# Grouped score products, a pinned TensorE order and slot weights spread by DMA in a fused Nyström attention and soft mixture-of-experts kernel

## The chip, the cores and the metric

One NeuronCore of a Trainium2 chip runs the whole kernel. The metric is device time in microseconds (us) of that core. The engines have names that the profile shortens: PE is TensorE (matrix products), PEld its weight loads, DVE is VectorE, ACT is ScalarE, POOL is GpSimd, SP is SyncE, which issues the DMAs. PSUM is the memory that TensorE writes; it has eight banks, and here each tile in it takes one bank.

## The reference, cut to what matters

```python
# q, k, v: (8 batches, 8 heads, 576 tokens, 64)
q_lm, k_lm = means of q and k over 32 segments of 18 tokens
A, Bm, C = sm(q, k_lm), sm(q_lm, k_lm), sm(q_lm, k)
Z = Bm.T / (norms of Bm)
for _ in range(6): Z = 2 * Z - Z @ Bm @ Z
x = A @ Z @ C @ v                       # then (8*576, 512)
g = x @ w_gate
x = (g * sigmoid(g) * (x @ w_val)) @ w_out
logits = x @ phi                        # 32 slots
d = softmax(logits, axis=0); slot_input = d.T @ x
slot_out[e] = relu(slot_input[e] @ w1[e]) @ w2[e]
out = softmax(logits, axis=1) @ slot_out
```

## The kernel before, in words

The eight batches run one after the other. In each, the feed-forward part dominates: for 12 blocks `j` of 128 hidden channels and 2 halves of 288 tokens, `unit` (L906) forms one gate group `pg` and one value group `pv` of six products each (`mm3`, L897: high and low halves of `E`, the softmax of A, times those of `G`). ACT turns `pg` into `u` (L917, L920), DVE multiplies `u` by `pv` into `hT` (L930, L932) and transposes `hT` into the big buffer `HB` (L761). `g_product` (L702) forms the `G` of two blocks at a time from `WB` and the weights: two PSUM tiles of tag "x", which ACT casts into `GH` (L727) and DVE subtracts into `GL` (L741).

Around these groups, work of other kinds is placed by slots. A batch has 48 slots, four per block `j`: after pg of half 0, after pv of half 0, after pg of half 1, after pv of half 1. In the second of the four (slot number 4j + 1) the `G` product of the next pair, where one is due, and the logits `l` of the previous block (L756) are always placed. Four generators are advanced at the slots which the lists in `SCHED` give them:

- `attention(b)` (L532, lists at1, at2, at3) prepares batch b during batch b - 1, so a negative slot lies in the batch before that. It has 34 steps: eight landmark sums on DVE (`landmark`, L319: four of k into `ks`, then four of q into `qs`), with the loads of the next q or k issued on SP after the fourth of each; four evictions of the A scores `m_a` by DVE (L547); four of the C scores `m_c` by ACT (L560); maxima and exponentials (L571 to L579); transposes `m_t` (L594 to L603); the product with v, `m_v` (L613); six steps of the Newton iteration, `m_n` (L634 to L658); and `m_w`, which gives `WB` (L519), after POOL has added the identity to `bd` (L659). q and k share four buffers: k is loaded for its landmarks, then q for landmarks and A scores, then k again for the C scores.
- `a_softmax(b)` (L664, lists am1 to am3) is the softmax of A, on DVE, POOL and ACT.
- `softmoe(b)` (L792, list sm) does the slot softmax of batch b during batch b + 1. Its weights `DN` lie transposed, and every group of 32 partitions needs those of all four groups. L839 to L844 spread them by eight recorded products `m_dr` into PSUM and by copies of DVE and ACT into `DR`. Then 144 small products `m_d` (L872) sum the tokens into four PSUM tiles (three of tag "x", one of tag "pv"), which DVE adds to `Sacc` (L882); these additions set a fence, and landmarks that come after them in the program wait for it.

The PSUM banks are three of tag "x", two of "pg", two of "pv" and one "l". In `attention` the scores of each half are one group: two "x" tiles, 16 products, two evictions (L541 to L561). So A and C scores stand in four places.

The framework's planner sets the order of instructions on each engine at compile time. It takes the earliest of the program that is ready by its own estimates, so work is moved ahead of the program's order where it expects an engine to be free. On the chip each engine then goes through its instructions in that fixed order. `issue_after` keeps an instruction behind another on its engine. `in_order` (L295) keeps exponentials and SiLUs apart, as a change between them loads an activation table; the halves in `TANH` (L939), which lie between the exponentials, use tanh instead.

The batch before the first (`first_attention`, L351) and the tail from L1091 on, the experts' products and the output, stand apart.

Of the kernel before, what the change touches and what calls it, by code (L numbers as in the profile page):

```python
# [19 lines left out]
M = 32  # L20
# [3 lines left out]
HALF = S // 2  # L24
NE, FF = 8, 1024
SEG = S // M
# [27 lines left out]
def nystrom_softmoe_kernel(  # L54
# [13 lines left out]
):  # L68
    nc = tc.nc
    pe, act, dve, pool, sp = nc.tensor, nc.scalar, nc.vector, nc.gpsimd, nc.sync  # L70

    def open_pool(name, bufs=1, **kw):
        return ctx.enter_context(tc.tile_pool(name=name, bufs=bufs, **kw))
# [30 lines left out]
    DN = cp.tile([128, 5, M], F32, name="DN")  # L104
# [188 lines left out]
    fence = {}  # L293
# [45 lines left out]
        E_t[b] = r  # L339

    def attention_tiles(b):
        ks = ap.tile([128, 4, M], F32, tag="ks", name="ks")
        qs = ap.tile([128, 4, M], F32, tag="qs", name="qs")
        if b != 1:
            e_tiles(b)
        AN = [ap.tile([128, SEG, M], F32, tag=f"AN{q}", name=f"AN{q}") for q in range(2)]
        A_t[b] = (AN, ap.tile([128, 2, SEG], F32, tag="mxA", name="mxA"))
        CE = [ap.tile([128, S + M], F32, tag=f"CE{q}", name=f"CE{q}") for q in range(2)]
        return ks, qs, AN, CE

    def first_attention(side):  # L351
        b = 0
        ks, qs, AN, CE = attention_tiles(b)
        NBUF = big("w5", "newton").rearrange("p (i q m) -> p i q m", q=2, m=128)
        am = [[psp.tile([128, 512], F32, tag=("pg", "pv")[half], name="m_a", bufs=2) for r in range(2)]
              for half in range(2)]
# [173 lines left out]
                          qk_t[nm, b, hp][64 * r:64 * r + 64, HALF * half:HALF * half + HALF], start=True, stop=True)  # L530

    def attention(b):  # L532
        assert b == 1 or ("att", b - 1) in seq
        ks, qs, AN, CE = attention_tiles(b)
        for nm, dst in (("k", ks), ("q", qs)):
            for hp in range(4):
                (landmark_pool if b == 1 and S_["lp"][2 * hp + (nm == "q")] else landmark)(nm, b, hp, dst)
                if hp == 3 and b > 1:
                    load_four("q" if nm == "k" else "k", b)
                yield  # L540
        for half in range(2):  # L541
            ms = [psp.tile([128, 512], F32, tag="x", name="m_a", bufs=3) for r in range(2)]
            scores(ms, ks, "q", b, half, range(4))
            assert b == 1 or ("asm", b - 1) in seq
            seq.add(("A", b, half))
            for r in range(2):
                dve.transpose(AN[r][:, 9 * half:9 * half + 9, :], ms[r][:, 0:HALF].rearrange("p (t r) -> p t r", r=32))  # L547
                yield
        for half in range(2):
            ms = [psp.tile([128, 512], F32, tag="x", name="m_c", bufs=3) for r in range(2)]  # L550
            scores(ms, qs, "k", b, half, range(4))
            n = HALF
            if half:
                n += M
                for hp in range(4):
                    for r in range(2):
                        pe.matmul(ms[r][32 * hp:32 * hp + 32, HALF:n], qs[64 * r:64 * r + 64, hp, :],
                                  ks[64 * r:64 * r + 64, hp, :], start=True, stop=True)
            for r in range(2):
                act.copy(CE[r][:, HALF * half:HALF * half + n], ms[r][:, 0:n])  # L560
                yield  # L561
        if b == 1:
            e_tiles(b)
        elif b < nb - 1:
# [5 lines left out]
        for q in range(2):  # L570
            dve.tensor_reduce(stat[:, q, 0:1], CE[q][:, 0:S], axis=AX.X, op=ALU.max)  # L571
            dve.tensor_reduce(stat[:, q, 1:2], CE[q][:, S:S + M], axis=AX.X, op=ALU.max)
            dve.tensor_scalar(stat[:, q, 2:3], stat[:, q, 0:1], -SC / SEG, None, ALU.mult)
            dve.tensor_scalar(stat[:, q, 3:4], stat[:, q, 1:2], -SC / (SEG * SEG), None, ALU.mult)
            yield
            in_order("exp", CE[q][:, 0:S], CE[q][:, 0:S], AF.Exp, bias=stat[:, q, 2:3], scale=SC / SEG,
                           accum_out=stat[:, q, 4:5])
            in_order("exp", CE[q][:, S:S + M], CE[q][:, S:S + M], AF.Exp, bias=stat[:, q, 3:4],
                           scale=SC / (SEG * SEG), accum_out=stat[:, q, 5:6])  # L579
            yield  # L580
# [83 lines left out]
    def a_softmax(b, qs=(0, 1)):  # L664
        EH, EL = E_t[b]
        AN, mxA = A_t[b]

        assert b == 0 or ("A", b, 1) in seq
        bc = {q: mxA[:, q, :].unsqueeze(2).to_broadcast([128, SEG, M]) for q in qs}
        at = {}  # L670

        def inv(q):
            mx = mxA[:, q, :]
            dve.tensor_reduce(mx, AN[q], axis=AX.X, op=ALU.add)
            dve.tensor_scalar(mx, mx, 1e-9, None, ALU.add)
            dve.reciprocal(mx, mx)

        def back(q):
            at[q] = ap.tile([128, S], F32, tag="AT", name="AT", bufs=2)
            dve.transpose(at[q].rearrange("p (t r) -> p t r", r=32), AN[q])  # L680

        for f in (lambda q: dve.tensor_reduce(mxA[:, q, :], AN[q], axis=AX.X, op=ALU.max),  # L682
                  lambda q: pool.tensor_tensor(out=AN[q], in0=AN[q], in1=bc[q], op=ALU.subtract),  # L683
                  lambda q: in_order("exp", AN[q], AN[q], AF.Exp, scale=SC / SEG),
                  inv,
                  lambda q: pool.tensor_tensor(out=AN[q], in0=AN[q], in1=bc[q], op=ALU.mult),
                  back,
                  lambda q: act.copy(EH[:, q, :], at[q]),
                  lambda q: pool.tensor_tensor(out=EL[:, q, :], in0=at[q], in1=EH[:, q, :], op=ALU.subtract)):
# [102 lines left out]
    def softmoe(b):  # L792
# [43 lines left out]
        room = spare[(b + 1) % 2]  # L836
        if b < nb - 1:
            DR = room[:, 0:640].rearrange("p (g k s) -> p g k s", g=4, k=5)
            for g in range(4):  # L839
                m = psp.tile([128, 512], F32, tag="x", name="m_dr", bufs=3)  # L840
                pe.matmul(m[:, 0:160], msum[32 * g:32 * g + 32, :],
                          DN[32 * g:32 * g + 32].rearrange("p k s -> p (k s)"), start=True, stop=True)
                o = DR[:, g].rearrange("p k s -> p (k s)")
                act.copy(o, m[:, 0:160]) if g % 2 else dve.tensor_copy(o, m[:, 0:160])  # L844
            d_of = lambda a, g, k: DR[32 * a:32 * a + 32, g, k, :]
        else:

# [39 lines left out]
            if a == 0:  # L887
                yield
        yield
        dve.tensor_reduce(mx, c, axis=AX.X, op=ALU.add)  # L890
        dve.tensor_scalar(mx, mx, 1e-9, None, ALU.add)
        dve.reciprocal(mx, mx)
        dve.tensor_tensor(out=c, in0=c, in1=bc, op=ALU.mult)
        yield


# [39 lines left out]

    WARM = [3, 4, 3, 2, 2]

    TANH = {(4, 1), (5, 0), (5, 1)}  # L939
    GROUPS = [2, 2, 4, 8, 8, 8, 4]  # L940


# [82 lines left out]
    def tail_loads(b, n):  # L1025
# [3 lines left out]
            for t in range(NW):  # L1029
                ffn_prefetch(t)  # L1030
        if b == last:
            if n == 25:
                for t in range(NW, NW + 3):
                    ffn_prefetch(t)
            if n % 8 == 6:
# [9 lines left out]
    for a in range(1, nb):  # L1045
# [5 lines left out]
        for r in S_["sm"]:  # L1051
            todo[48 * a + r].append(sm)
    prev = None
    for b in range(nb):
        for j in range(NJ):
            p = prev
            def slot(i):
# [24 lines left out]
                if not first:  # L1082
                    for gen in todo[48 * b + n]:
                        next(gen, None)
                if n == 46 and b + 1 < nb:
                    g_unit(b + 1, 0)
                if n == 47:
                    g_low()

            prev = (b, j, *unit(b, j, slot))  # L1090
    in_order("exp", warm, one, AF.Exp)  # L1091
    logits(*prev)
    transposes(*prev)
# [205 lines left out]
```

## Time and profile before

| | |
|---|---|
| time of the kernel, median of 3 runs | 687.33 us (687.18 to 689.19) |
| time of the profiled execution | 688.07 us |
| its span, first to last instruction | 686.3 us |
| PE busy | 641.6 us, 93% |
| DVE busy | 484.5 us, 71% |
| ACT busy | 307.2 us, 45% |
| POOL busy | 72.2 us, 11% |
| mean granted TensorE clock | 0.985 of 2.4 GHz |

Busy time of PE counts each product from its start to its modelled end, and products overlap in the pipeline. So the time that a group costs is read from the start of its first product to the start of the next group, and a small gap inside "busy" does not show as idle. The time of the profiled execution is 1.77 us over its span and 0.74 us over the median.

### The profile page before, as it was taken

What the parts mean: (1) busy time and instruction counts of PE and PEld (TensorE: products, weight loads), DVE (VectorE), ACT (ScalarE), POOL (GpSimd) and SP (SyncE); (2) the same over time, 40 slices, a digit from 0 to 9 for tenths busy, and PEclk for the clock granted to TensorE, in tenths of its full rate; (3) what the DMA queues carried; (4) which work ended last, traced back from release to release, by engine and by line L of the source; (5) the groups of instructions that cost most, each with busy time, mean ns of one, the idle gap of its engine ahead of it and who ended that gap; (6) DMA issues with size and microseconds to landing.
All of it is one profiled execution on the core that took longest, in us unless ns stands there. A gap on an engine that the chain in (4) does not pass through costs nothing.

```text
span 686.3 us, 18326 instructions
## 1 busy us (share of the span) xinstructions
PE 641.6 (93%) x7639; PEld 470.2 (69%) x7639; DVE 484.5 (71%) x1166; ACT 307.2 (45%) x776; POOL 72.2 (11%) x81
## 2 busy tenths in 40 slices
PE   5699999999999999999999999999999999989991
PEld 2576767776877687777777777777768886843560
DVE  4999989878657985798569856976696655550441
ACT  2566875356335533463246324632364342321441
POOL 0401012012001200120012001200130000010000
PEclk9799999999999999999999999999999999999996
DMA  7788773232203230224022402240212296789999
GB/s 283 258 323 316 279 269 119 83 126 84 70 1 96 72 114 2 72 82 126 1 71 71 140 1 70 72 139 1 71 63 63 77 367 227 249 268 351 348 369 326
DMA packets 59843, 105.01 MB, mean 153 GB/s; under 512 B 3824, under 2 KB 29552, under 8 KB 58224
## 3 DMA queue, kind: packets, MB, share of 16 engines
q1 hardware_dynamic: 59760, 103.84, 45.0%
q8 instruction: 60, 0.98, 0.6%
q14 instruction: 23, 0.19, 0.1%
HBM read 91.24 MB, written 12.58 MB: 151 GB/s over the span
## 4 chain that ended last, share of the span: by engine, by line
PE 68%; DVE 17%; ACT 6%; DMA 4%; issue 2%; POOL 1%; SPq 0%; POOLq 0%; ACTq 0%; DVEq 0%
PE pg L903 20%; PE pv L903 17%; PE g L710 6%; PE l L756 4%; PE m_n L637 3%; PE m_d L872 3%; PE m_f L1232 2%; PE m_f L1184 2%; PE m_a L529 2%; DMA q<-in_qT_dram 2%; DMA v<-in_v_dram 2%; DVE bd L311 2%; DVE GL L741 1%; DVE Sacc L882 1%; DVE qs L322 1%
## 5 line engine op out<-in xcount | busy, mean ns | idle before, releaser
L301 ACT ACTIVATE u<-pg 128x288 f32<-128x288 f32 x174 | 71.4, 411 | 143.8 <-PE pg L903 138.7
L932 DVE TENSOR_TENSOR hT<-u,pv 128x288 f32<-128x288 f32 x174 | 78.2, 450 | 56.9 <-PE pv L903 51.3
L903 PE MATMUL pg<-EH,GH 128*128 128x288 f32 x384 | 96.9, 330 | 2.5 <-ACT GH L727 1.6
L741 DVE TENSOR_TENSOR GL<-g,GH 128x512 fp32r<-128x512 f32 (+1 forms) x122 | 66.0, 571 | 38.7 <-ACT GH L727 38.5
L903 PE MATMUL pv<-EH,GH 128*128 128x288 f32 x384 | 91.2, 312 | 0.5 <-DVE hT L932 0.5
L903 PE MATMUL pg<-EH,GL 128*128 128x288 f32 x384 | 86.0, 299 | 0.0
L903 PE MATMUL pg<-EL,GH 128*128 128x288 f32 x384 | 84.0, 298 | 0.0
L903 PE MATMUL pv<-EH,GL 128*128 128x288 f32 x384 | 83.1, 295 | 0.0
L903 PE MATMUL pv<-EL,GH 128*128 128x288 f32 x384 | 82.7, 296 | 0.0
L727 ACT CAST GH<-g 128x512 fp32r<-128x512 f32 (+1 forms) x122 | 54.2, 496 | 56.4 <-PE g L710 56.3
L903 PEld LDWEIGHTS pg<-EH,GH 128*128 128x128 f32 x384 | 59.9, 189 | 25.3 <-issue 20.3
L761 DVE STREAM_TRANSPOSE HB<-hT 128x576 f32<-128x576 f32 x96 | 73.9, 770 | 1.3
L903 PEld LDWEIGHTS pv<-EH,GH 128*128 128x128 f32 x384 | 61.4, 188 | 18.0 <-issue 16.2
L903 PEld LDWEIGHTS pg<-EH,GL 128*128 128x128 f32 x384 | 62.3, 188 | 2.2 <-issue 2.1
L903 PEld LDWEIGHTS pg<-EL,GH 128*128 128x128 f32 x384 | 61.6, 188 | 1.8 <-issue 1.8
L903 PEld LDWEIGHTS pv<-EL,GH 128*128 128x128 f32 x384 | 61.6, 188 | 0.9 <-issue 0.9
L903 PEld LDWEIGHTS pv<-EH,GL 128*128 128x128 f32 x384 | 61.9, 188 | 0.5 <-issue 0.5
L710 PE MATMUL g<-w,WB 64*32 64x512 f32 (+1 forms) x976 | 56.5, 510 | 0.4 <-ACT WB L523 0.4
L756 PE MATMUL l<-hT,P_sb 128*32 128x128 f32 (+1 forms) x768 | 47.4, 298 | 0.7 <-DVE hT L932 0.6
L756 PEld LDWEIGHTS l<-hT,P_sb 128*32 128x32 f32 x768 | 15.9, 108 | 40.3 <-issue 17.8
L872 PE MATMUL m_d<-HB,HB 32*32 32x384 f32 x1116 | 39.5, 491 | 0.3 <-DVE GL L741 0.3
L683 POOL TENSOR_TENSOR AN<-AN,mxA 128x576 f32<-128x576 f32 x16 | 18.4, 1170 | 179.6 <-DVE mxA L682 163.3
(248 smaller groups left out, 945.2 us busy)
## 6 DMA issues: line engine op xcount, KB each, us to landing
k<-in_kT_dram SPq DMA_DIRECT2D x52, 288.0 KB, 3.8
ffn<-in_w_dram SPq DMA_DIRECT2D x13, 1024.0 KB, 8.7
ffn<-in_w_dram SPq DMA_DIRECT2D x24, 512.0 KB, 8.8
HB<-in_w_cat_dram SPq DMA_DIRECT2D x8, 1024.0 KB, 7.8
v<-in_v_dram SPq DMA_DIRECT2D x8, 1024.0 KB, 6.0
q<-in_qT_dram SPq DMA_DIRECT2D x28, 288.0 KB, 3.2
HB<-in_w_out_dram SPq DMA_DIRECT2D x12, 512.0 KB, 5.8
wr<-in_w_cat_dram SPq DMA_DIRECT2D x4, 1024.0 KB, 9.4
```

The costliest lines, as they stand in the source:

```text
L301: i = act.activation(*a, **kw)
L311: dve.tensor_tensor(out=dst[:, q, :].rearrange("p (h m) -> p h m", h=4), in0=src.unsqueeze(1).to_broadcast([128, 4, 32]), in1=bm3, op=ALU. ...
L637: pe.matmul(m[:, 96 * q:96 * q + 96], bd[:, q, :], RV[:, q, :], start=True, stop=True)
L683: lambda q: pool.tensor_tensor(out=AN[q], in0=AN[q], in1=bc[q], op=ALU.subtract),
L710: pe.matmul(gs[r][32 * hp:32 * hp + 32, 0:256 * n].rearrange("p (u f) -> p u f", u=n), WB[b % 2][64 * r:64 * r + 64, hp, :], w[64 * r:64 * ...
L727: act.copy(H_, g)
L741: dve.tensor_tensor(out=GL, in0=g, in1=GH, op=ALU.subtract)
L756: pe.matmul(L[32 * c:32 * c + 32, 0:32 * k], P_sb[:, j, :], main[:, 0:k, c, :], start=j == 0, stop=j == NJ - 1)
L761: dve.transpose(HB[b % 2][:, S * j:S * j + S].rearrange("p (t r) -> p t r", r=32), hT[:, 0:S].rearrange("p (t r) -> p t r", r=32))
L872: pe.matmul(ms[a][32 * g:32 * g + 32, 0:384].rearrange("p (j f) -> p j f", j=NJ), d_of(a, g, k), hb[32 * a:32 * a + 32, :, 4 * k + g, :], ...
L903: pe.matmul(ps[:, 0:HALF], G_t[b, j, q, sel_][h], e[:, q, ts_], start=n == 0, stop=n == 5)
L932: dve.tensor_tensor(out=o, in0=u, in1=pv[:, 0:HALF], op=ALU.mult)
```

## The change

The score products of both halves of A are formed in one group of 32, and those of C likewise, for batches from 2 on; the fourth PSUM tile is taken from tag "pv" and evicted first. The order of all PE instructions from batch 1 to the end of batch 7 is tied to the program's order (`keep_order`). In `softmoe` of batches 0 to 5, twelve DMAs on SP copy `DN` into `DR`, and the group that a partition already holds is read from `DN`; `softmoe(6)` keeps the products. The slots of nearly all steps change; landmarks of batches from 3 on may begin before the attention of the batch before has ended; the first `G` product of the next batch moves from slot 46 to 45; the tanh halves move with the exponentials. Two fences are added on DVE.

```diff
-    'at2': [-3, -2, -1, 0, 3, 4, 5, 6, 8, 8, 10, 10, 16, 16, 18, 18, 19, 20, 20, 21, 22, 23, 25, 26, 27, 28, 29, 31, 33, 35, 37, 39, 41, 43],
-    'am2': [11, 11, 12, 12, 18, 19, 21, 22, 23, 25, 27, 29, 31, 32, 34, 36, 37],
-    'at3': [-3, -2, -1, 0, 3, 4, 5, 6, 8, 8, 10, 10, 16, 16, 18, 18, 19, 20, 20, 21, 22, 23, 25, 26, 27, 28, 29, 31, 33, 35, 37, 39, 41, 43],
-    'am3': [11, 11, 12, 12, 18, 19, 21, 22, 23, 25, 27, 29, 31, 32, 34, 36, 37],
-    'sm': [1, 3, 10, 17, 19, 20, 23, 24, 24, 27],
+    'at2': [-3, -2, -1, 0, 1, 2, 3, 4, 5, 6, 6, 7, 9, 10, 10, 11, 11, 12, 13, 13, 14, 14, 17, 17, 17, 18, 21, 23, 24, 28, 30, 32, 34, 37],
+    'am2': [7, 7, 8, 8, 12, 13, 15, 16, 17, 19, 21, 23, 25, 27, 29, 31, 33],
+    'at3': [-11, -10, -9, -8, -5, -4, -3, -2, 1, 2, 2, 3, 9, 10, 10, 11, 11, 12, 13, 13, 14, 14, 17, 17, 17, 18, 21, 23, 24, 28, 30, 32, 34, 37],
+    'am3': [6, 7, 7, 8, 12, 13, 15, 16, 17, 19, 21, 23, 25, 27, 29, 31, 33],
+    'sm': [2, 3, 5, 9, 10, 10, 25, 26, 26, 28],
...
+    def keep_order(engine, start, end):
+        last = None
+        for i in nc.cur_bb.bb.instructions[start:end]:
+            if i.engine == engine:
+                if last is not None:
+                    tc.add_manual_dep(i, last.name, mybir.DependencyInfo(
+                        mybir.DependencyClass.NoSync, mybir.DependencyReason.DATA), reason="keep_order")
+                last = i
...
     def attention(b):
-        assert b == 1 or ("att", b - 1) in seq
+        assert b == 1 or ("q", b - 1) in seq
...
+        def score_tiles(name):
+            ms = [psp.tile([128, 512], F32, tag="pv" if i == 3 else "x", name=name, bufs=2 if i == 3 else 3)
+                  for i in (3, 0, 1, 2)]
+            return {(1, 1): ms[0], (0, 0): ms[1], (0, 1): ms[2], (1, 0): ms[3]}
+        together = b > 1
...
+            if together:
+                t = score_tiles(name)
+                for half in (1, 0):
+                    product(half, [t[half, 0], t[half, 1]])
+                for half, r in ((1, 1), (0, 0), (0, 1), (1, 0)):
+                    eviction(half, r, t[half, r])
+                    yield
...
-            dve.tensor_scalar(stat[:, q, 3:4], stat[:, q, 1:2], -SC / (SEG * SEG), None, ALU.mult)
+            i = dve.tensor_scalar(stat[:, q, 3:4], stat[:, q, 1:2], -SC / (SEG * SEG), None, ALU.mult)
+            fence["stat"] = getattr(i, "ins", i)
...
-            dve.tensor_reduce(mx, AN[q], axis=AX.X, op=ALU.add)
+            with tc.issue_after(fence["stat"]) if b > 1 else nullcontext():
+                dve.tensor_reduce(mx, AN[q], axis=AX.X, op=ALU.add)
...
-            for g in range(4):
+            for i in range(1, 4 if b < nb - 2 else 1):
+                for a in range(4):
+                    sp.dma_start(DR[32 * a:32 * a + 32, a ^ i], DN[32 * (a ^ i):32 * (a ^ i) + 32])
+            for g in range(4 if b == nb - 2 else 0):
                 m = psp.tile([128, 512], F32, tag="x", name="m_dr", bufs=3)
...
-            d_of = lambda a, g, k: DR[32 * a:32 * a + 32, g, k, :]
+            d_of = lambda a, g, k: (DN if a == g else DR[:, g])[32 * a:32 * a + 32, k, :]
...
-        dve.tensor_reduce(mx, c, axis=AX.X, op=ALU.add)
...
+        with tc.issue_after(fence["sum"]):
+            dve.tensor_reduce(mx, c, axis=AX.X, op=ALU.add)
...
-    TANH = {(4, 1), (5, 0), (5, 1)}
+    TANH = {(2, 1), (3, 0), (3, 1)}
...
-            if n == 25:
+            if n == 26:
                 for t in range(NW, NW + 3):
                     ffn_prefetch(t)
...
-                if n == 46 and b + 1 < nb:
+                if n == (46 if b == 0 else 45) and b + 1 < nb:
                     g_unit(b + 1, 0)
-                if n == 47:
+                if n == (47 if b == 0 else 46):
                     g_low()
...
+    keep_order(mybir.EngineType.PE, middle, n_ins())
```

## Rows read from the trace of the kernel before

**Rows 1.** The chain that ended last: start us, us, what; a batch apart

```profile
217.27 1.28 ACT L301
...
287.02 1.28 ACT L301
...
356.94 1.28 ACT L301
...
506.65 4.95 PE m_d L872 x141
...
571.22 4.25 PE m_d L872 x141
```

**Rows 2.** Busy time by engine in the stretch of one batch

```profile
core 0: us, PE busy (x) PEld busy (x) DVE busy (x) ACT busy (x) POOL busy (x), PEclk, DMA share, GB/s
...
287.02:356.94 69.92, 68.65 (x842) 51.97 (x832) 53.30 (x129) 30.69 (x79) 8.25 (x8) 1.00 0.22 69
```

**Rows 3.** Waits of PE, 224 to 502 us: us in total, times, longest

```profile
PE m_n L637 <- ACT RV L644: 2.8, 4, 0.8
PE m_w L522 <- POOL bd L659: 1.5, 4, 0.4
```

**Rows 4.** Timeline of PE, 354.7 to 358.5 us: start, us, engine, line, operation

```profile
354.73 0.43 PE L903 MATMUL pv<-EH,GH 128*128 128x288 f32 x2
...
355.52 0.43 PE L903 MATMUL pg<-EH,GH 128*128 128x288 f32 x2
...
356.41 0.71 PE L529 MATMUL m_c<-k,qs 64*32 64x288 f32 x16
357.05 0.53 PE L903 MATMUL pv<-EH,GH 128*128 128x288 f32 x2
...
358.05 0.47 PE L756 MATMUL l<-hT,P_sb 128*32 128x160 f32 x8
358.44 0.53 PE L903 MATMUL pg<-EH,GH 128*128 128x288 f32 x2
```

**Rows 5.** Timeline of PE around the spread of the slot weights

```profile
292.24 0.55 PE L841 MATMUL m_dr<-DN,cst 32*128 32x160 f32 x6
...
293.20 0.53 PE L841 MATMUL m_dr<-DN,cst 32*128 32x160 f32 x2
...
294.52 1.09 PE L710 MATMUL g<-w,WB 64*32 64x512 f32 x16
```

**Rows 6.** Timeline of PE at the end of a batch

```profile
334.11 1.09 PE L710 MATMUL g<-w,WB 64*32 64x512 f32 x16
335.13 0.53 PE L903 MATMUL pv<-EH,GH 128*128 128x288 f32 x2
...
339.67 0.42 PE L903 MATMUL pv<-EH,GH 128*128 128x288 f32 x2
```

**Rows 7.** Timeline of PE, Newton steps and the product after them

```profile
316.31 0.47 PE L756 MATMUL l<-hT,P_sb 128*32 128x160 f32 x8
317.58 0.66 PE L637 MATMUL m_n<-RV,bd 128*128 128x96 f32 x4 [0.80 <-ACT RV L644]
...
319.70 0.58 PE L637 MATMUL m_n<-RV,bd 128*128 128x96 f32 x4
...
330.84 0.44 PE L522 MATMUL m_w<-bd,VD 128*64 128x128 f32 x4 [0.36 <-POOL bd L659]
```

**Rows 8.** Timeline of DVE beside these steps

```profile
311.76 1.50 DVE L322 TENSOR_REDUCE qs<-q 128x32 f32<-128x576 f32 x2 [0.48 <-DMA q<-in_qT_dram]
...
318.27 0.49 DVE L311 TENSOR_TENSOR bd<-m_n,cst 128x128 f32<-128x128 f32 x2 [0.28 <-PE m_n L637]
...
319.10 0.29 DVE L653 TENSOR_TENSOR RV<-RV,m_n 128x128 f32<-128x128 f32 x1 [0.33 <-ACT RV L652]
```

**Rows 9.** Timeline of SP: one load of k as four DMAs

```profile
290.50 1.75 SPq L149 DMA_DIRECT2D k<-in_kT_dram  x4
```

**Rows 10.** DMA issues: times, KB each, median us to landing

```profile
k<-in_kT_dram SPq DMA_DIRECT2D x52, 288.0 KB, 3.8
```

**Rows 11.** Groups by line, whole kernel: the evictions of the A scores

```profile
L547 DVE STREAM_TRANSPOSE AN<-m_a 128x288 f32<-128x288 f32 x28 | 11.9, 463 | 11.7 <-PE m_a L529 11.7
```

More of the change, by code (lines that the diff above doesn't have):

```diff
@@ L341, in attention_tiles @@
     def attention_tiles(b):
[L342 to L345, printed above, removed]
         AN = [ap.tile([128, SEG, M], F32, tag=f"AN{q}", name=f"AN{q}") for q in range(2)]
@@ L348, in attention_tiles, with landmark_tiles @@
         CE = [ap.tile([128, S + M], F32, tag=f"CE{q}", name=f"CE{q}") for q in range(2)]
-        return ks, qs, AN, CE
+        return AN, CE
+    def landmark_tiles():
+        return ap.tile([128, 4, M], F32, tag="ks", name="ks"), ap.tile([128, 4, M], F32, tag="qs", name="qs")
     def first_attention(side):
         b = 0
-        ks, qs, AN, CE = attention_tiles(b)
+        ks, qs = landmark_tiles()
+        e_tiles(b)
+        AN, CE = attention_tiles(b)
         NBUF = big("w5", "newton").rearrange("p (i q m) -> p i q m", q=2, m=128)
@@ L532, in attention @@
     def attention(b):
-        assert b == 1 or ("att", b - 1) in seq
-        ks, qs, AN, CE = attention_tiles(b)
+        assert b == 1 or ("q", b - 1) in seq
+        ks, qs = landmark_tiles()
         for nm, dst in (("k", ks), ("q", qs)):
@@ L540, in attention @@
                 yield
[L541 to L550, printed above, removed]
+        def score_tiles(name):
+            ms = [psp.tile([128, 512], F32, tag="pv" if i == 3 else "x", name=name, bufs=2 if i == 3 else 3)
+                  for i in (3, 0, 1, 2)]
+            return {(1, 1): ms[0], (0, 0): ms[1], (0, 1): ms[2], (1, 0): ms[3]}
@@ L551, in attention, with a_eviction, c_product @@
+        together = b > 1
+        assert b == 1 or ("att", b - 1) in seq and ("asm", b - 1) in seq
+        AN, CE = attention_tiles(b)
+        if b != 1:
+            e_tiles(b)
+        def a_eviction(half, r, m):
+            dve.transpose(AN[r][:, 9 * half:9 * half + 9, :], m[:, 0:HALF].rearrange("p (t r) -> p t r", r=32))
+            if (half, r) == (1, 0 if together else 1):
+                seq.add(("A", b, 1))
+        def c_product(half, ms):
             scores(ms, qs, "k", b, half, range(4))
-            n = HALF
@@ L553, in attention, with c_eviction @@
             if half:
-                n += M
                 for hp in range(4):
                     for r in range(2):
-                        pe.matmul(ms[r][32 * hp:32 * hp + 32, HALF:n], qs[64 * r:64 * r + 64, hp, :],
+                        pe.matmul(ms[r][32 * hp:32 * hp + 32, HALF:HALF + M], qs[64 * r:64 * r + 64, hp, :],
                                   ks[64 * r:64 * r + 64, hp, :], start=True, stop=True)
-            for r in range(2):
-                act.copy(CE[r][:, HALF * half:HALF * half + n], ms[r][:, 0:n])
-                yield
+        def c_eviction(half, r, m):
+            n = HALF + M * half
+            act.copy(CE[r][:, HALF * half:HALF * half + n], m[:, 0:n])
@@ new lines, in attention @@
+        for name, product, eviction in (
+                ("m_a", lambda half, ms: scores(ms, ks, "q", b, half, range(4)), a_eviction),
+                ("m_c", c_product, c_eviction)):
+            if together:
[5 more added lines that the diff above has]
+                    yield
+            else:
+                for half in range(2):
+                    ms = [psp.tile([128, 512], F32, tag="x", name=name, bufs=3) for r in range(2)]
+                    product(half, ms)
+                    for r in range(2):
+                        eviction(half, r, ms[r])
+                        yield
@@ L889, in softmoe @@
         yield
-        dve.tensor_reduce(mx, c, axis=AX.X, op=ALU.add)
-        dve.tensor_scalar(mx, mx, 1e-9, None, ALU.add)
-        dve.reciprocal(mx, mx)
-        dve.tensor_tensor(out=c, in0=c, in1=bc, op=ALU.mult)
+        with tc.issue_after(fence["sum"]):
+            dve.tensor_reduce(mx, c, axis=AX.X, op=ALU.add)
+            dve.tensor_scalar(mx, mx, 1e-9, None, ALU.add)
+            dve.reciprocal(mx, mx)
+            dve.tensor_tensor(out=c, in0=c, in1=bc, op=ALU.mult)
         yield
@@ L1053, in nystrom_softmoe_kernel @@
     prev = None
+    n_ins = lambda: len(nc.cur_bb.bb.instructions)
     for b in range(nb):
+        if b == 1:
+            middle = n_ins()
         for j in range(NJ):
```

## The prediction

> **What bounds the kernel now.** I read the chain that ended last first. One table load returns in it once a batch, and the distance is the length of a batch in the steady middle: 69.75 and 69.92 us [rows 1]. From the m_d of batch 6 to that of batch 7 it is 64.57 us, as batch 7 prepares no further attention. The stretch of one batch comes next: PE is busy for 68.65 of 69.92 us at full clock, DVE for 53.30, ACT for 30.69 [rows 2]. So the middle is bound by PE, with DVE at 76% behind it. The waits of PE over four batches hold only two that come back, on the Newton step and on the product after it: 2.8 and 1.5 us, or 0.7 and 0.4 us a batch [rows 3]. There is little idle time to win; what can be won is PE's own time. For that I read its timeline from start to start. A plain group of six takes 0.79 us (354.73 to 355.52). With a foreign product behind it, it takes 0.89 (355.52 to 356.41), and with one on either side 1.00 (357.05 to 358.05) [rows 4]. So each place where other work is put between pg and pv costs 0.2 us beyond that work.
>
> Here the rule and the rows differ in size. The Trainium skill (TensorEngine Tiling (Array Packing), Key Properties) says that a change of tiling mode drains the array, and TensorE: Matmul & The Clock Gate (Step-by-step: what each phase is for) gives about 128 cycles for a drain. Two changes at 2.4 GHz would be an estimated 0.11 us, half of what the rows show; the seven places below would then give 0.7 us a batch in place of 1.4, and the sum would end near 673 us. The measurement decides.
>
> **The change part by part**, for a steady batch (2 to 5), a slot being 69.92/48 = 1.46 us [rows 2].
>
> 1. Slot weights by DMA. The eight m_dr stand in two pieces with a pv group cut between them; from the first of them to the next g it takes 2.28 us [rows 5]. The pv group alone, with g behind it, is 0.89, and the pg before loses its 0.09 of change [rows 4]. PE saves 2.28 - 0.89 + 0.09 = 1.5 us. DVE and ACT lose two copies each, which frees no path by itself. Added are twelve DMAs at slot 10; m_d stands at slot 25, 15 slots or 21.8 us later. Four loads are issued in 1.75 us [rows 9], so twelve take 5.3 us, and one of 288 KB lands 3.8 us after issue [rows 10]: 9.1 us, hidden. Copies within SBUF are in no row; below that lies the issue alone, above it a landing one after another, 12 x 3.8 = 45.6 us, 24 us too late. I take the first, since the four loads go out side by side. On SP the twelve wait for DN, and behind them stands the load of the next k (slot 11), whose landmarks stand at slot 37; that cover is 38 us.
>
> 2. Fewer places. Counted in the timeline of one batch, 13 pieces stand alone between pg and pv: A scores 2, C scores 2, m_d 1, m_t 2, m_n 4, m_w 1, g of the next batch 1. In the new lists, scores (slots 1 and 9), m_t (17), m_v (21), m_d (25), m_w (37) and g (45) all fall on slots 4j + 1, beside the logits that stand there anyway. Alone remain the six m_n (23, 24, 28, 30, 32, 34). Seven places fewer at 0.2 us [rows 4]: 1.4 us. The merged scores are half of the first four of these.
>
> 3. The end of a batch. With g at slot 46 only one pv stands between g and the first pg of the next batch, and the planner has shuffled pg, pv and l: from 335.13 to 339.67 it takes 4.54 us [rows 6]. Four plain groups, one l (0.39) and the changes around both pieces would be 3.16 + 0.39 + 0.3 = 3.85 [rows 4]. The new place, with two groups between, saves 0.7 us.
>
> 4. The old waits. l at 316.31 is followed by a late m_n, 0.80 us idle [rows 7], since DVE stood at q landmarks that waited for a load [rows 8]. Landmarks move away from the Newton steps in the program and m_w gets three slots. Both waits go: 0.7 + 0.4 = 1.1 us [rows 3].
>
> Gross 1.5 + 1.4 + 0.7 + 1.1 = 4.7 us a batch.
>
> 5. New waits, because PE can't be sent around a late product. What is late next is the Newton chain. From the start of one m_n, bd ends 1.2 and RV 1.81 us later (317.58 to 319.39) [rows 7, 8]. Between steps 0 and 1 (slots 23, 24) only m_n itself and one pg stand, 0.36 + 0.89 = 1.25 us: a wait of 0.55. It is nothing at best, and 1.3 if a landmark of 0.75 us is ahead on DVE (1.50 for two [rows 8]). m_d, one slot later, needs the bank of step 1: 0.2 (0 to 0.6). Steps 3 to 4 have one m_n and two groups, 2.05 us: 0.25 (0 to 0.75). Other places 0.2 (0 to 0.85). Sum 1.2, between 0 and 3.5; I take it since it lies near the durations that the rows show for these same steps. Behind a waiting m_n stand pg and pv, and behind these ACT and DVE.
>
> 6. Nothing from the fourth bank. The A evictions take 4 x 0.46 = 1.85 us on DVE [rows 11], but the pv bank is emptied first, and pg, pv, pg (2.4 us) stand before the next pv that needs it; the "x" banks are wanted at slots 5 and 13, four slots on. If that cover went, PE would wait about 0.46 us for each eviction. The two fences move DVE work alone, which waits for nobody on PE. The tanh halves move with the exponentials: nothing.
>
> Net 4.7 - 1.2 = 3.5 us a batch, 14.0 for batches 2 to 5. Batch 1 has no wait at step 1, so 4.0 gross; its q load has only one slot to its first landmark, so I put its new waits at 1.6: 2.4. Batch 6 has neither part 3 nor part 4: 2.9 less 0.9 (no landmarks run there) = 2.0. Batch 7 keeps the recorded spread; m_d joins l: 0.2. Batch 0 and the tail keep their work. Sum 18.6 us: 688.07 - 18.6 = 669.5 for the profiled execution. That lies 0.74 us over the median of 687.33, so I forecast 669.
>
> **The rivals.**
>
> Smaller gain. The four banks are held longer than part 6 has it, because DVE, already 76% busy, would be 81% busy over 66 us and the planner puts other work ahead of the evictions. If PE waits for two evictions at each of the two places (4 x 0.46 = 1.8 us a batch), the net is 1.7: 4 x 1.7 + 0.6 + 0.2 + 0.2 = 7.8 us, 679. For it: DVE's length of queue is not seen by PE's pinned order. Against: now DVE waits for the scores, 11.7 us in all, not PE for DVE [rows 11].
>
> No new waits. The Newton steps arrive in time, as most do now: 4 x 4.7 + 4.0 + 2.9 + 0.2 = 25.9 us, 661.
>
> Slower: the pin and a late landmark. The fence lets landmarks start after Sacc (slot 26), and the planner may again move them ahead, now into the Newton steps of slots 28 to 34. If it sends q landmarks before a step's bd, DVE stands until the load lands, 3.8 us [rows 10], and then sums four tiles, 3.0 us [rows 8]. PE has about 2.0 us of groups to go on with, and waits 4.8. The net is then 4.7 - 1.2 - 4.8 = -1.3 in batches 2 to 5, about -2.4 in batch 1: 7.6 lost, 2.2 won in batches 6 and 7, 693. It decides from 3.5 us of wait a batch on. For it: this happened at 311.76 and cost 0.8 [rows 7, 8]. Against: DVE's idle time there was only 0.48, since other work filled the load's time. The Trainium skill (TensorE: Matmul & The Clock Gate, The mechanism) says that products start and end strictly in program order, which speaks against pinning where data may be late; the trace agrees: at 316.31 nothing passes the late m_n.
>
> **How the numbers follow.** Forecast 0.58, smaller gain 0.18, no new waits 0.13, slower 0.11. The range takes in the bounds of part 5: 661 with none; with all at their upper end 4 x 1.2 + 0.5 + 0.4 + 0.2 = 5.9 us, 681. For the price of a place, between 0.2 and a little more, I open it to 659, and toward the last rival to 684; what lies beyond on either side is left out. About 0.3%, 2 us, is what a measurement of this kernel can tell from no change. Faster 0.87: the first three without the edge of the second; same 0.04, that edge; slower 0.09.
>
> **What would show it.** In the profile after: table loads about 66.4 us apart; no m_dr but in batch 7; scores as 32 products beside l; no shuffled pg and pv at a batch's end; PE's waits led by m_n at step 1, under 1.5 us each, none at m_d for a DMA. I am wrong if PE waits over 3.5 us a batch, for bd, RV, HB or evictions, or if a batch stays at 69 us with no waits, which would mean that places cost nothing.

## The result and the profile after

Four runs of the changed kernel took 680.82 us in the median (679.62 to 682.29), four of the kernel before on the same chip 687.35 (687.18 to 689.19): a ratio of 0.990 [0.9873, 0.9927]. It is faster, as forecast, and the time lies in the range; but 6.5 us were gained where 18.3 were forecast. The profiled executions stand at 688.07 and 681.4 us, 6.7 apart; the account below is made between these.

First the length of every batch, worked out from the traces as the time from the start of a batch's first `u` on ACT (the 1st, 25th, 49th and so on; 268.58 to 338.50 us for batch 3 of the kernel before) to that of the next. Batch 7 is counted to the start of its last `u`, and the tail runs from there to the end of the span. The 42.61 us ahead of the first `u`, 42.70 after the change, are not in the table.

| us | batch 0 | 1 | 2 | 3 | 4 | 5 | 6 | 7 | tail |
|---|---|---|---|---|---|---|---|---|---|
| before | 85.35 | 70.89 | 69.74 | 69.92 | 69.22 | 69.96 | 66.59 | 56.29 | 85.74 |
| after | 85.23 | 71.11 | 68.07 | 68.03 | 68.07 | 68.03 | 66.35 | 57.07 | 84.93 |
| gained | 0.1 | -0.2 | 1.7 | 1.9 | 1.2 | 1.9 | 0.2 | -0.8 | 0.8 |
| forecast | 0 | 2.4 | 3.5 | 3.5 | 3.5 | 3.5 | 2.0 | 0.2 | 0 |

A batch from 2 to 5 gained about half of its forecast; batches 1, 6 and 7 together gained nothing. Busy time in one batch, from one table load to the next, answers to [rows 2]:

```profile
core 0: us, PE busy (x) PEld busy (x) DVE busy (x) ACT busy (x) POOL busy (x), PEclk, DMA share, GB/s
277.25:345.29 68.04, 65.67 (x826) 51.28 (x825) 51.26 (x127) 29.34 (x77) 8.28 (x8) 1.00 0.23 75
```

PE's busy time fell by 2.98 us and its idle time rose from 1.27 to 2.37: work was saved, and part of it came back as waiting. The waits of PE over four batches (199 to 471 us: in total, times, longest) answer to [rows 3]:

```profile
PE m_n L673 <- DVE RV L689: 5.2, 4, 1.3
PE pg L944 <- DVE GL L778: 1.6, 8, 0.2
PE m_n L673 <- DVE bd L321: 1.3, 2, 0.7
PE m_n L673 <- ACT u L311: 1.3, 2, 0.6
```

No wait for a DMA and none at m_d. m_n waits for RV once in each batch, once more for bd or u by turns, and pg waits for GL. They are followed up in the timeline of all engines, here of batch 3 (start, us, engine, line, operation):

```profile
285.32 0.72 DVE L711 TENSOR_REDUCE mxA<-AN 128x18 f32<-128x576 f32 x1
285.78 0.42 PE L944 MATMUL pg<-EH,GH 128*128 128x288 f32 x2
285.96 1.28 DVE L778 TENSOR_TENSOR GL<-g,GH 128x512 fp32r<-128x512 f32 x2
287.53 0.43 PE L944 MATMUL pv<-EH,GH 128*128 128x288 f32 x2
...
298.12 0.58 PE L673 MATMUL m_n<-RV,bd 128*128 128x96 f32 x4
298.48 0.51 PE L944 MATMUL pg<-EH,GH 128*128 128x288 f32 x2
300.17 0.66 PE L673 MATMUL m_n<-RV,bd 128*128 128x96 f32 x4 [0.66 <-DVE bd L321]
...
301.96 0.51 PE L912 MATMUL m_d<-HB,DN 32*32 32x384 f32 x1
...
306.67 0.53 PE L944 MATMUL pg<-EH,GH 128*128 128x288 f32 x2
...
308.37 0.42 PE L944 MATMUL pg<-EH,GH 128*128 128x288 f32 x2
...
309.15 0.58 PE L673 MATMUL m_n<-RV,bd 128*128 128x96 f32 x4
...
312.15 1.37 DVE L332 TENSOR_REDUCE ks<-k 128x32 f32<-128x576 f32 x2
312.79 0.58 PE L673 MATMUL m_n<-RV,bd 128*128 128x96 f32 x4
313.44 1.28 DVE L778 TENSOR_TENSOR GL<-g,GH 128x512 fp32r<-128x512 f32 x2
314.02 0.43 PE L944 MATMUL pg<-EH,GH 128*128 128x288 f32 x2
314.63 0.48 DVE L321 TENSOR_TENSOR bd<-m_n,cst 128x128 f32<-128x128 f32 x2
315.03 0.44 DVE L973 TENSOR_TENSOR hT<-u,pv 128x288 f32<-128x288 f32 x1
315.39 0.74 DVE L332 TENSOR_REDUCE ks<-k 128x32 f32<-128x576 f32 x1
316.06 0.28 DVE L689 TENSOR_TENSOR RV<-RV,m_n 128x128 f32<-128x128 f32 x1
316.48 0.66 PE L673 MATMUL m_n<-RV,bd 128*128 128x96 f32 x4 [1.30 <-DVE RV L689]
```

Read from start to start, a group of six with a foreign product on one side takes 0.88 us, and against that all three waits are counted, here and in the expectations. It fits the second. The first stands between groups of its own kind, and the third has only an m_n behind it, which costs the group ahead nothing: the pg of 308.37 takes 0.78. So the first and the third are rather 0.1 us longer each, and the sum 3.4 us in place of 3.3.

- 285.78 to 287.53, 1.75 us: 0.87 of wait. GL is late: DVE first sums a row of A (L711), and the cast GH before it ends on ACT only at 285.57, behind the exponentials of C.
- 298.48 to 300.17, 1.69 us: 0.81, the step from Newton product 0 to 1.
- 314.02 to 316.48, 2.46 us: 1.58, the step from 3 to 4. From 312.15 on DVE does two k landmarks, GL, bd, hT and a third landmark before RV, which the m_n of 316.48 asks for. In the program these landmarks stand at slots 37 and later; the planner took them ahead into the Newton steps.

Together 3.3 us of new waits a batch. m_d takes 4.71 us (301.96 to 306.67) and waits for nothing.

Batch 1 has waits of its own (timeline of PE, 134 to 154 us):

```profile
134.95 1.31 PE L540 MATMUL m_a<-q,ks 64*32 64x288 f32 x16 [0.41 <-DVE GL L778]
141.58 1.11 PE L540 MATMUL m_c<-k,qs 64*32 64x288 f32 x6 [0.94 <-DMA k<-in_kT_dram]
153.09 0.47 PE L793 MATMUL l<-hT,P_sb 128*32 128x160 f32 x8 [1.15 <-DVE hT L971]
```

### The profile page after: what moved, and what is told of

The parts are those of the page before. It is cut to its first block, busy times and chain, and to the rows that moved or that the text cites. A ratio compares the mean times of both kernels' runs of the same rounds, so it can differ in the third digit from the quotient of the medians.

```text
span 679.6 us, 18326 instructions
## 1 busy us (share of the span) xinstructions
PE 627.6 (92%) x7591; PEld 467.3 (69%) x7591; DVE 473.1 (70%) x1154; ACT 300.7 (44%) x764; POOL 72.4 (11%) x81
## 5 line engine op out<-in xcount | busy, mean ns | idle before, releaser
L944 PE MATMUL pg<-EH,GH 128*128 128x288 f32 x384 | 94.1, 324 | 2.6 <-ACT GH L764 1.6
L944 PE MATMUL pv<-EH,GH 128*128 128x288 f32 x384 | 86.4, 304 | 0.0
L778 DVE TENSOR_TENSOR GL<-g,GH 128x512 fp32r<-128x512 f32 (+1 forms) x122 | 64.8, 570 | 26.0 <-ACT GH L764 25.9
L793 PE MATMUL l<-hT,P_sb 128*32 128x160 f32 (+1 forms) x768 | 45.2, 298 | 1.8 <-DVE hT L971 1.1
L912 PE MATMUL m_d<-HB,DN 32*32 32x384 f32 x288 | 37.2, 491 | 0.0
```

Of the source, the lines that this page charges most:

```text
L778: dve.tensor_tensor(out=GL, in0=g, in1=GH, op=ALU.subtract)
L793: pe.matmul(L[32 * c:32 * c + 32, 0:32 * k], P_sb[:, j, :], main[:, 0:k, c, :], start=j == 0, stop=j == NJ - 1)
L912: pe.matmul(ms[a][32 * g:32 * g + 32, 0:384].rearrange("p (j f) -> p j f", j=NJ), d_of(a, g, k), hb[32 * a:32 * a + 32, :, 4 * k + g, :], ...
L944: pe.matmul(ps[:, 0:HALF], G_t[b, j, q, sel_][h], e[:, q, ts_], start=n == 0, stop=n == 5)
```

## The experiments

Steady means batches 2 to 5. Each ratio is to the kernel before, on the same chip; the change itself stands at 0.990 [0.9873, 0.9927].

**Where the new wait comes from.** First (e4) the landmarks are held back by a fence behind the last Newton step.

```diff
-        with tc.issue_after(fence["sum"]) if "sum" in fence else nullcontext():
+        f = fence.get("newton", fence.get("sum"))
+        with tc.issue_after(f) if f is not None else nullcontext():
...
-                    dve.tensor_tensor(out=VD, in0=m3[:, :, 32:96], in1=RV[:, :, 32:96], op=ALU.add)
+                    i = dve.tensor_tensor(out=VD, in0=m3[:, :, 32:96], in1=RV[:, :, 32:96], op=ALU.add)
+                    fence["newton"] = getattr(i, "ins", i)
```

> The changed kernel, with the landmarks on DVE kept behind the last Newton step of the batch before in the program. Theory (landmarks sent ahead by the planner stand between the Newton steps on DVE and make PE wait 1.57 us before step 4 in each of batches 2 to 5): that wait falls below 0.4 us, 5 to 8 us less, 673 to 676 us. Rival (step 4 is late since only two groups stand before it and GL is ahead of it on DVE in any case): under 2 us less, 679 to 682. It can also be lost again if q lands late for the next batch: then PE waits at the scores.

674.38 us, 0.9786 [0.9762, 0.9811]. A steady batch takes 66.6 us, 1.45 less. Its timeline (PE and DVE) at the same step:

```profile
309.06 1.29 DVE L780 TENSOR_TENSOR GL<-g,GH 128x512 fp32r<-128x512 f32 x2
309.57 0.58 PE L674 MATMUL m_n<-RV,bd 128*128 128x96 f32 x4
...
311.45 0.28 DVE L690 TENSOR_TENSOR RV<-RV,m_n 128x128 f32<-128x128 f32 x1
311.78 0.69 PE L674 MATMUL m_n<-RV,bd 128*128 128x96 f32 x4
...
315.73 0.74 DVE L333 TENSOR_REDUCE ks<-k 128x32 f32<-128x576 f32 x1
```

From m_n to m_n it is 2.21 us in place of 3.69, with GL still in between: the landmarks made 1.48 us of the wait, and 0.1 to 0.2 us are left. In PE's waits m_n for RV is gone, and the other three lines stay as they were.

**The pin.** The change without `keep_order` (e1):

```diff
-    keep_order(mybir.EngineType.PE, middle, n_ins())
```

> The changed kernel without the tie of the TensorE order; lists, merged scores and DMAs stay. Theory (the pin itself costs little; the lost time lies in DVE, which reaches the Newton steps and GL late): the planner is free again and sends other groups past some late steps, so within 2 us of the changed kernel, 679 to 683 us. Rival (the pin holds PE behind late products, 3.3 us a batch): the waits at the Newton steps go and the time falls by over 5 us, below 676. If the planner's own order is bad, as at the end of a batch before: above 685.

678.26 us, 0.9848 [0.9814, 0.9882]. Steady 66.63 us, as short as with the fence; of PE's waits only pg for GL stays (1.6 us in four batches). The wait before step 1 is gone too, but it brought nothing beyond what the fence brings: the planner sends a pv ahead of that m_n, cuts the m_n and l into pieces, and m_d takes 5.10 us (302.75 to 307.85) in place of 4.71. And batch 1 takes 73.76 us, 2.65 more: there the planner cuts a late m_n into the m_d. So in these lists the pin costs 1.4 us a steady batch, as PE stands where it was sent before, and saves 2.65 us once. The Trainium skill (TensorE: Matmul & The Clock Gate, The mechanism) has products start and end in program order, and the rows agree: nothing passes the m_n of 316.48. By that rule a pin is as good as its list is timely.

The pin alone, on the kernel before (e7):

```diff
+        if b == 1:
+            middle = n_ins()
...
+    keep_order(mybir.EngineType.PE, middle, n_ins())
```

> The kernel before with the order of TensorE tied to the program's from batch 1 on, and nothing else. Theory (tying gains nothing by itself: the shuffle at the end of a batch is the planner's way around a late GH, and without it PE waits there; late Newton steps hold it too): 688 to 695 us. Rival (the tie ends the shuffle and saves the 0.7 us a batch that it was thought to cost): 682 to 685.

692.85 us, 1.0073 [1.0046, 1.01]: slower, 0.7 us a steady batch. PE's waits, 199 to 465 us:

```profile
PE m_dr L851 <- ACT HB L854: 1.6, 4, 0.4
PE pg L913 <- DVE GL L751: 1.6, 4, 0.4
PE m_d L882 <- DVE GL L751: 1.5, 4, 0.4
PE m_n L647 <- DVE RV L663: 0.9, 3, 0.3
```

The wait on pg is the end of a batch: g at slot 46, GL not there in time for the first pg. By this the shuffle of pg, pv and l in [rows 6] was the planner's way round a late GL. In the changed kernel the groups after that g (332.46 us on) come in order and without a wait, and so they do in e1 without the pin (332.10 us on): slot 45, not the pin, made the shuffle needless.

**The parts of the saving.** The scores split into halves again, all else as changed (e3):

```diff
-        together = b > 1
+        together = False
```

> The changed kernel, with the scores of each half in a group of its own again and no score tile in a pv bank. Theory (a place between pg and pv costs 0.2 us): one place more for A and one for C in batches 1 to 5, 0.4 us a batch for five batches, 2 us slower, 682 to 684. Rival (the merged group holds banks and costs as much as it saves): within 0.7 us of the changed kernel or faster. A wait for the second group's banks would come on top, above 685.

693.56 us, 1.0075 [1.005, 1.0101]: slower than before. Steady 69.4 to 69.8 us, 1.5 more than after; batch 1, where the places of these lists are closer, 78.06, 7 more. Its timeline of PE:

```profile
344.60 0.72 PE L540 MATMUL m_a<-q,ks 64*32 64x288 f32 x16
345.25 0.53 PE L944 MATMUL pg<-EH,GH 128*128 128x288 f32 x2
...
346.24 0.97 PE L540 MATMUL m_a<-q,ks 64*32 64x288 f32 x16
347.13 0.54 PE L944 MATMUL pv<-EH,GH 128*128 128x288 f32 x2
```

The second group of A costs a place of its own (pg 345.25 to 346.24: 0.99 against 0.79) and waits for its banks (0.89 us for 16 products where the first 16 took 0.65). The waits show l behind a late hT besides, 2.5 us in four batches. Merging is thus worth more than its two places, 0.4 us, because it also asks for its banks once; how much of the 1.5 us comes from lists made for the merged group is not shown. The 0.2 us of a place is confirmed for the scores. By the estimate of 0.11 us that the prediction made from two pages of the Trainium skill (TensorEngine Tiling (Array Packing), Key Properties; TensorE: Matmul & The Clock Gate, Step-by-step: what each phase is for) that pg would have taken 0.90; the measurement decides.

A place of m_n costs half as much. The rows write its products as 128*128, like those of pg and pv: the group ahead of it takes 0.78 us (308.37 to 309.15, kernel after), as if alone, and the group behind it 0.87 (313.15 to 314.02). m_t shows the same 0.88 behind it (289.88 to 290.76). By this the seven places of the prediction's part 2 are an estimated 1.3 us in place of 1.4: six of m_a, m_c, m_d and g at 0.2 us, three of m_t and m_w less two of m_n at 0.1.

The spread by PE in all batches, at slot 10 and all else as changed (e2):

```diff
-            for i in range(1, 4 if b < nb - 2 else 1):
+            for i in range(1, 1):
...
-            for g in range(4 if b == nb - 2 else 0):
+            for g in range(4):
```

> The changed kernel, with the slot weights of all batches spread by recorded products and copies again, at slot 10, in place of the DMAs. Theory (this work costs PE 1.5 us a batch): six batches, 9 us slower, 688 to 692. As slot 10 lies right behind the C scores, which hold all x banks, waits for banks can add up to 1.5 us a batch, to 699. Rival (the place beside it hides much of it, or the DMAs cost something in turn): under 5 us slower.

702.55 us, 1.0196 [1.0171, 1.0221], above the upper end of what was expected: 2.9 to 4.9 us more a steady batch. Its timeline of PE:

```profile
287.40 0.53 PE L881 MATMUL m_dr<-DN,cst 32*128 32x160 f32 x2
288.15 0.83 PE L881 MATMUL m_dr<-DN,cst 32*128 32x160 f32 x4 [0.21 <-ACT CE L578]
289.54 0.53 PE L881 MATMUL m_dr<-DN,cst 32*128 32x160 f32 x2 [0.56 <-ACT HB L884]
```

In the new lists the eight products stand in the middle of the score copies and wait for ACT to empty their banks. This prices m_dr at a bad place, not in the kernel before; for that the spread is taken out of the kernel before itself (e5):

```diff
-            for g in range(4):
+            for g in range(0):
...
-            d_of = lambda a, g, k: DR[32 * a:32 * a + 32, g, k, :]
+            d_of = lambda a, g, k: DN[32 * a:32 * a + 32, k, :]
```

> The kernel before with the spread of the slot weights left out: no recorded products for it, no copies, and the sums over tokens read the weights of their own partitions only. Theory (it costs PE 1.5 us a batch in batches 1 to 7, as the starts in the timeline say): 10 us less, 676 to 679 us where the kernel before is at 687 to 688. Rival (freed PE time is lost again at the next late product, the Newton step): 4 to 7 us less.

684.47 us, 0.9947 [0.9928, 0.9965]: steady 0.45 us less on average, not 1.5. Timeline of PE:

```profile
295.79 0.83 PE L872 MATMUL m_d<-HB,DN 32*32 32x384 f32 x2
296.82 4.89 PE L872 MATMUL m_d<-HB,DN 32*32 32x384 f32 x142 [0.20 <-DVE GL L741]
301.64 0.54 PE L903 MATMUL pg<-EH,GH 128*128 128x288 f32 x2
```

m_d now takes 5.85 us where it took 4.83 before: with m_dr gone it comes too early for the bank that GL still reads. In the old lists 1.0 of the 1.5 us went into that wait. In the changed kernel m_d takes 4.71 us and waits for nothing, so nothing shows there that takes the 1.5 us back; no run prices m_dr alone at a good place in the new lists.

The changed kernel without its DMAs (e6):

```diff
-            for i in range(1, 4 if b < nb - 2 else 1):
+            for i in range(1, 1):
...
-            d_of = lambda a, g, k: (DN if a == g else DR[:, g])[32 * a:32 * a + 32, k, :]
+            d_of = lambda a, g, k: (DN if a == g or b < nb - 2 else DR[:, g])[32 * a:32 * a + 32, k, :]
```

> The changed kernel with its twelve DMAs left out in batches 0 to 5; the sums read the weights of their own partitions only. Theory (the DMAs are hidden: none of the sums waits for them): the same, within 1 us. Rival (SP is held for 6 to 8 us by their issue, so loads behind them come late, in batch 1 above all, or their packets slow others): 2 to 4 us less.

681.22 us, 0.9905 [0.9874, 0.9935], the same as the change: the twelve DMAs are hidden, though SP issues them for 7.49 us where 5.3 were estimated (timeline of SP, kernel after). The last of these has landed at 288.21, 13.8 us before m_d.

```profile
279.48 7.49 SPq L878 DMA_DIRECT2D HB<-DN  x12
```

**Can the rest be had?** All further runs build on the fence of e4. The transposes of the states, which run between the two RVs of step 0, are put behind that step's bd (e11):

```diff
+                fence["k0"] = getattr(i, "ins", i)
...
+        with tc.issue_after(fence["k0"]) if "k0" in fence else nullcontext():
+            dve.transpose(HB[b % 2][:, S * j:S * j + S].rearrange("p (t r) -> p t r", r=32),
...
```

> The kernel with late landmarks, with transposes of hT on DVE kept behind the masked copies of Newton step 0, and without the other order of the run with two. Theory (a transpose of 0.77 us between the two parts of step 0 on DVE makes the wait of 0.81 us before step 1): 0.2 to 0.6 us go in batches 1 to 6, 1 to 4 us less; the two orders together lost because of the one on the row sums of A. Rival (the wait only moves to the product behind, through ACT): within 1 us.

674.42 us, 0.98 [0.9777, 0.9823], as without it. The wait of 0.81 before step 1 moved into the product itself (timeline of PE and ACT):

```profile
297.00 0.43 PE L674 MATMUL m_n<-RV,bd 128*128 128x96 f32 x2
...
297.13 0.41 ACT L311 ACTIVATE u<-pg 128x288 f32<-128x288 f32 x1 [0.25 <-PE pg L948]
...
297.43 0.31 ACT L681 ACTIVATE RV<-m_n,rc 128x64 f32<-128x64 f32 x1
...
297.79 0.46 PE L674 MATMUL m_n<-RV,bd 128*128 128x96 f32 x2 [0.36 <-ACT RV L681]
...
298.04 0.51 PE L948 MATMUL pv<-EH,GH 128*128 128x288 f32 x2
```

m_n takes 1.04 us (297.00 to 298.04) in place of 0.43. The second half waits for RV from ACT, and ACT takes a `u` ahead of that RV. So the step's own chain, m_n to DVE and ACT to m_n, and the order on ACT both stand behind the wait; no run parts them.

The same, and the row sums of A behind GL as well (e8):

```diff
-            with tc.issue_after(fence["stat"]) if b > 1 else nullcontext():
+            with tc.issue_after(fence["stat"]) if b > 1 else nullcontext(), tc.issue_after(fence["gl"]) if b > 1 else nullcontext():
...
+            fence["gl"] = getattr(i, "ins", i)
```

> The kernel with late landmarks, and two orders more on DVE: transposes of hT behind the masked copies of Newton step 0, and the row sums of the A softmax behind the GL of the pair before. Theory (the other two waits of the changed kernel, 0.81 us before step 1 and 0.87 before the first pv of block 4, each in batches 1 to 6, come from work that DVE takes first): 0.5 us and 0.6 us of them go, six batches, 5 to 8 us less than with late landmarks alone, 667 to 670. Rival (the chain through PSUM and ACT sets them, not DVE's order): under 2 us less.

675.97 us, 0.9823 [0.9798, 0.9848]; steady 67.0 to 67.3, worse by 0.5 than e4. Its waits are led by m_n for ACT's RV (1.5 us in four batches) and pg for ACT's GH (1.2): moved on, not removed.

Four steps of the attention, the second long exponential of C among them, one slot on, so that GH comes sooner (e10):

```diff
-    'at3': [-11, ... 9, 10, 10, 11, 11, 12, 13, 13, 14, 14, 17, ...
+    'at3': [-11, ... 9, 10, 10, 11, 11, 12, 14, 14, 15, 15, 17, ...
```

> The kernel with late landmarks, with the last exponential of C and the two small steps behind it one slot later (slots 14 and 15 in place of 13 and 14) for batches from 3 on. Theory (the wait of 0.87 us at the GL of block 4 begins on ACT, which takes the exponentials before the cast GH): the cast comes first, and 0.5 to 0.9 us go in batches 2 to 6, 2 to 4 us less. Rival (it begins on DVE, which sums rows of A before it forms GL): under 1 us less.

673.78 us, 0.9788 [0.9762, 0.9814], the same as e4: the planner left that exponential ahead of the cast (280.99 and 281.76 us on ACT), so the question stayed open.

The attention of batch 2, which runs mostly in batch 1, with the list of the later batches, and its first load of k 11 slots earlier (e9):

```diff
-    'at2': [-3, -2, -1, 0, 1, 2, 3, 4, 5, 6, 6, 7, 9, ...
+    'at2': [-11, -10, -9, -8, -5, -4, -3, -2, 1, 2, 2, 3, 9, ...
...
-    'lq': 44,
+    'lq': 33,
```

> The kernel with late landmarks, and batch 1 given the same slots for its attention as the later batches (landmarks from slot -11, A scores at slot 1), with the first load of k for batch 2 issued at slot 33 of batch 0 in place of 44. Theory (batch 1 loses 2.4 us because A scores at slot 5 wait for banks that g holds, and C scores at slot 9 for the reload of k): batch 1 goes from 70.5 to about 68 us, 2 to 3.5 us less in all. Rival (batch 0 grows by what batch 1 saves, since its DVE is full with the conversion of the weights): within 1 us.

672.29 us, 0.9763 [0.9743, 0.9784]. Batch 1 takes 67.27 us against 70.52 in e4, batch 0 1.5 more. The waits of m_a, for a bank that GL still read, and of m_c, for k, are gone; the run moves the slots and the load together, so it does not part the two.

This kernel with the second long exponential of C fenced behind the cast to GH (e12):

```diff
+            with tc.issue_after(fence["gh"]) if q and b > 1 else nullcontext():
+                in_order("exp", CE[q][:, 0:S], CE[q][:, 0:S], AF.Exp, bias=stat[:, q, 2:3], scale=SC / SEG,
...
+            i = act.copy(H_, g)
+            fence["gh"] = getattr(i, "ins", i)
```

> The kernel with late landmarks and early loads, with the second long exponential of C kept behind the cast GH of the pair before it on ACT. Theory (the wait of 0.87 us at the GL of block 4 begins with the 0.78 us of this exponential, taken ahead of the cast): about 0.7 us a batch go in batches 1 to 6, 3 to 5 us less than with early loads alone, 667 to 669. Rival (DVE, which sums rows of A for 0.72 us ahead of GL, sets it alone): within 1 us.

675.55 us, 0.981 [0.9793, 0.9826]; steady 67.1, 0.5 more than e9. Timeline of ACT and DVE:

```profile
279.74 1.08 ACT L767 CAST GH<-g 128x512 fp32r<-128x512 f32 x2
281.13 0.75 DVE L714 TENSOR_REDUCE mxA<-AN 128x18 f32<-128x576 f32 x1
281.79 1.28 DVE L782 TENSOR_TENSOR GL<-g,GH 128x512 fp32r<-128x512 f32 x2
```

The cast has ended at 280.82, GL begins 0.97 us later: here it is DVE's queue that keeps GL, not ACT. The 0.5 us are a new wait: PE waits 2.1 us in four batches for hT at l (199 to 465 us), which the kernel after does not, as the pv before that l takes 1.49 us (283.36 to 284.85) in place of 0.89.

And e9 without the pin (e13):

```diff
-    keep_order(mybir.EngineType.PE, middle, n_ins())
```

> The kernel with late landmarks and early loads, without the tie of the TensorE order. Theory (tying pays nothing once nothing late stands in the program's order, and costs nothing either): within 2 us of the kernel with early loads, 670 to 674. Rival (the planner's own order is worse, as in batch 1 of the run without the tie): over 675. Third (it passes the two waits that are left): under 668.

671.18 us, 0.9747 [0.9732, 0.9761]. The interval overlaps that of e9: once landmarks keep out of the Newton steps and batch 1 is in order, the pin neither costs nor saves what can be told. The wait before step 1 is gone from PE's list here as well, yet a steady batch is only 0.16 us shorter than in e9 (66.45 against 66.61), since m_n and l are cut and m_d takes 5.10 us again. Both e9 and e13 beat the change and the kernel before.

## Why the prediction was right and wrong

**Parts 1 to 4, the gross saving: right.** After, a steady batch takes 68.05 us on average, 69.71 before; without its new waits it would take 64.8 (64.6 with the longer reading of the waits), so 4.9 to 5.1 us were saved where 4.7 were forecast. m_dr, the single places but those of m_n, the shuffle and both old waits are gone from the steady batches. Three reasons were wrong in detail: m_dr can be worth 1.5 us only in lists that also move m_d (in the old ones it was 0.45), merging the scores brought more than its places, and a place of m_n, m_t or m_w costs 0.1 us, not 0.2. That the sum comes out so near is thus luck in part.

**Part 5, new waits of 1.2 us: the step that failed.** They come to 3.3. "Steps 3 to 4 have one m_n and two groups, 2.05 us: 0.25 (0 to 0.75)" measured 1.58, twice its own upper end. It counted the Newton chain alone on DVE, with an upper end as long as one landmark, 0.75 us. But DVE's order is the planner's, and three landmarks and a GL, 3.4 us by their rows, stood in it. The fence shows that 1.45 us of it was the landmarks. Of the other terms, step 0 to 1 measured 0.81 (0.55; 0 to 1.3), m_d none (0.2), the other places 0.87 (0.2; 0 to 0.85), all of this a late GL. So 2.1 us too many a batch, less 0.2 more of gross: 1.8 short in each of four batches, 7.4 of the 11.9 us that are missing. That the waits still lie inside the 0 to 3.5 us of the sum, and the time inside its range, is luck too: the bounds of the other terms made room for the one that was wrong.

**The slower rival had the mechanism, at a third of its price.** It sent landmarks of q ahead into the Newton steps with a load still on its way: 4.8 us. What came were landmarks of k, already loaded: 1.6. It was given 0.11 and priced only with the load's wait; without that wait the bounds of the sum had room for one landmark at a step, and three came. The rival for a smaller gain came nearest in time, 679 us, for a reason that isn't there: no PE wait is for an eviction of scores.

**Batch 1: 1.6 us of new waits became about 6.** Worked out from start to start: against a steady batch m_a takes 1.2 us longer, m_c 2.2, l comes 1.15 behind hT, and the step to m_n 1 takes 1.5 longer. The prediction put 1.6 us there for the late q load, but none of these waits is for that load: m_a waits for a bank that GL still reads, m_c for the reload of k, and ahead of the step to m_n 1 DVE sums two landmarks of q that the planner took ahead (161.65, 1.40 us). The fence of e4 took 0.6 us of that step (batch 1: 70.52), and e9 took back 3.3 us more and lost 1.5 in batch 0. By the gross of 4.0 the batch would have lost 2 us; it lost 0.2. Some 1.2 us of the difference are waits of the kernel before in this batch, which that gross left out: a pg of 1.57 us in place of 0.88 ahead of a pv that waits for hT (167.93), and m_d 5.38 in place of 4.83. The rest stays open.

**Batches 6 and 7.** Batch 6 keeps two of the waits, 0.87 and 0.81 us, where the prediction put the new waits at 0.9 in all because no landmark runs there: neither of the two is a landmark's. That is 0.8 of the 1.8 us that are missing there; the rest stays open. In batch 7 m_d takes 5.20 us in place of 4.25 [rows 1]: it now stands right behind a g whose banks GL still holds, the wait that e5 showed (weight loads of m_d wait 0.7 us for GL). The tail's 0.8 us for the better says nothing: the tails of the runs above, which hardly differ in it, lie between 84.5 and 86.4 us.

**Right as well:** the DMAs cost nothing, the fourth bank costs nothing, and a place of scores costs 0.2 us. Not settled: whether the waits of 0.87 and 0.81 us can be had as time; e8, e11 and e12 moved them, e10 did not reach them, and in e1 and e13 the second went without the batch growing shorter by as much.

## What to carry to other kernels

When an engine's order is pinned, write down for every product what it waits for and everything that the other engine's scheduler may put ahead of that, not the dependency chain alone; work whose data is there early is just what a scheduler hoists. A removed stretch of one engine's work is worth its length only if what follows can start sooner: in the kernel before, m_d then waited for its bank, and 1.0 of 1.5 us was lost. And a fence at the one place where hoisted work hurts was worth 1.45 us a batch here, as much as giving up the pin.

## What the runs showed of the hardware

Thirty-two products of A in one group take 1.13 us, less than twice the 0.65 of sixteen in e3 (timeline of PE, kernel after):

```profile
268.20 1.20 PE L540 MATMUL m_a<-q,ks 64*32 64x288 f32 x32
269.33 0.53 PE L944 MATMUL pg<-EH,GH 128*128 128x288 f32 x2
```

And twelve small copies within SBUF keep SP issuing for 7.49 us, 0.62 each, where four loads of k took 1.75 [rows 9], 0.44 each, and 2.22 right behind the copies (287.08, kernel after).

In the trace of before, one pair of bd of RV takes 2.10 us on DVE (301.47) and another 0.48 (317.15): beside the first POOL works on EL (300.58, 2.85 us), beside the second POOL is idle. It is so in each of batches 2 to 6. The Trainium skill (GPSIMD Engine Reference, Specifications) says that GpSimd shares its SBUF interfaces with VectorE and that they contend where a VectorE operation has two SBUF inputs; these rows agree.
